# Moved scalings and sink products, a table for the rank comparisons, gated weight loads and more idle products in a sink-window attention with top-1 experts

## The chip, the cores and the metric

The kernel runs on one core of one Trainium2 chip. The metric is the device time of one execution in microseconds (us); a run's figure is the median over its executions, and the document compares medians. One execution was recorded by the hardware profiler; its rows give every duration used below.

## What is computed

The reference is attention with four sink columns and a window of 128, followed by a mixture of experts with one expert per token and a capacity of 80 tokens per expert.

```python
# q, k, v: (4, 8, 768, 64); n_sink = 4, window = 128
scores = scale * np.matmul(q, k.transpose(0, 1, 3, 2))
keep = is_sink | in_window
scores = np.where(keep, scores, -1000000000.0)
a = softmax(scores)                       # max subtracted, sum + 1e-9
x = matmul(a, v) -> (3072, 512)           # tokens by (head, dim)
logits = x @ w_gate                       # 8 experts
expert_idx = argmax(logits); gate_w = softmax(logits)[expert_idx]
for e in range(8):
    tok_idx = tokens of expert e, at most 80, those of the largest gate_w
    h = relu(x[tok_idx] @ w1[e])          # 512 -> 1024
    out[tok_idx] = gate_w[tok_idx, None] * (h @ w2[e])
```

Rows of tokens that are not chosen stay zero.

## The kernel before

The attention part is 48 ticks, each for one pair of query blocks (128 rows) with one pair of heads. Everything in it is in an order written out by hand, the same for all engines: the loop over `n` at line 972 calls, per tick, the scores of tick `n`, the transposes of tick `n - 1`, the weighted sums of tick `n - 2`, and between them the stages of a calendar. `at(key, f, ...)` puts a call into the calendar, `run(n, stage)` runs what is due at that stage of tick `n`. Each engine takes its instructions in that order, so an instruction that waits holds everything behind it on its engine.

In one tick TensorE makes the score products (`scores`, line 581), VectorE masks them and takes the row maxima (`softmax`, lines 599 to 609), ScalarE exponentiates (`exps`, line 619), GpSimd spreads the four sink probabilities into `stk` (`sink_probs`, line 627), and TensorE transposes the probabilities (line 635) and `stk` (`sinks_turn`, line 639). ScalarE copies both out of PSUM (lines 642 and 646), GpSimd masks the copies (lines 654 and 661), and TensorE makes the weighted sums (line 687).

The queries of the first four ticks arrive as four separate transfers (`first_pair`). Each is multiplied by 0.125 on GpSimd (`scale_first`, line 484): numbers 0 and 1 before the ticks, 2 and 3 at the very end of ticks 1 and 2. The gate logits ride on the weighted sums as eight extra value columns. They are made by `value_logits` (line 432) for the values and by `sink_logits` (line 446) for the sink rows. `sink_keep` (line 451) copies the sink part into `vst_raw`, and `round_v` and `split_v` (lines 411, 415) make `vst` from it, which tick 2's weighted sums read.

Gate keys of a token tile are ready some three ticks after its last scores (`gate_terms`, `gate_logits`, `gate_exp`, `gate_hit`, `gate_keys`). `keys_turn` and `keys_keep` lay them out as a row `krow`. A token's rank within its expert is found by comparing its key with all earlier keys, in pieces of up to 768 columns per tile `i`; 60 pieces in all. A piece is done on VectorE (`rank_compare`, lines 827 and 830) or on ScalarE (`rank_sign`, line 845); GpSimd then rescales the ScalarE results (`sign_settle`, line 853), and TensorE sums the other side of each comparison into `cnt` (`rank_count`, line 863). Waiting pieces stand in the list `rank_todo`. In the ticks before, VectorE takes up to two pieces per tick, at most a fifth of the list rounded up, and from tick 32 on ScalarE takes one per tick. Seven pieces are left when the ticks end. They and the last tiles' pieces are done in the tail, lines 1028 to 1117. The tail ends in a loop over what is left (line 1101), with `ot` (GpSimd, line 1095), its sum `os` (VectorE, line 1106) and `base` (GpSimd, line 1107) for the offsets of the experts, and with the sum `rsum` (line 1116) and the subtraction that gives `rank` (line 1117). `keep_warm(n)` issues `n` products whose result nobody reads (line 970).

The selection compares ranks with slots (line 1141), and 24 products (line 1144) turn that into token numbers. Then 14 products that nobody reads follow (line 1161). GpSimd gathers the tokens of expert 0 and 1 from memory (line 1164). For each expert, `tokens` scales the gathered rows on VectorE (line 1201) and transposes them (line 1203), `ffn1` (line 1219) and `ffn2` (line 1240) multiply by the weights, and `rows` writes the output.

Weights come as 32 halves of 1 MB on the SyncE queue, through `load_weight` (line 304). The first 12 go out during the ticks. The loop right behind the attention part (line 1125) asks for four more, numbers 12 to 15: number 12 goes to the last third of the tile `kv`, 13 to 15 to buffers of the pool `wpool3`, whose memory the attention part used before. Number 16 goes to its fourth buffer.

## Time and profile before

| | us |
|---|---|
| median of three runs | 303.65 |
| lowest and highest run | 301.45, 304.17 |
| profiled execution | 305.9 |
| its span, first to last instruction | 304.2 |
| around the span | 1.7 |

The profiled execution is 2.25 us above the median. Its mean granted clock of TensorE is 0.953 of full speed. In the span the first score product starts at 6.30 us, the ticks and the tail reach to the rank at 195.70 us, the first expert's products start at 206.84 us, and the last output transfer is issued at 299.56 us.

### The profile page before, as it was taken

The numbers are of one execution on the slowest core, as the hardware profiler recorded it, in microseconds if no ns is written. First come the engines' busy times: TensorE is split into PE (matmuls) and PEld (weight loads), VectorE is DVE, ScalarE is ACT, GpSimd is POOL, SyncE is SP. The second block draws the span as 40 slices with busy tenths as digits, with TensorE's granted clock in tenths as the row PEclk, the third lists the DMA queues.
The fourth block names the chain that finished last, engine by engine and source line by source line (L and its number), as shares of the span: only waits on it lengthen the run. The fifth ranks groups of instructions, "written<-read, shape, count | busy, mean of one in ns | idle before, by whom it ended". The sixth has DMA issues, their size and how long they took to land.

```text
span 304.2 us, 13249 instructions
## 1 busy us (share of the span) xinstructions
PE 267.5 (88%) x5407; PEld 219.5 (72%) x5407; DVE 165.7 (54%) x508; ACT 165.4 (54%) x652; POOL 138.6 (46%) x365
## 2 busy tenths in 40 slices
PE   8769999999999998999899977478899997998991
PEld 3557787777787766786777756348898986997980
DVE  5666858688688969879878899702301101100001
ACT  1566668887779876989999968300112211211210
POOL 4336557756598654568956747432112201011111
PEclk9989999999999999999999999557999999799997
DMA  7996976194961799999998997891766968358401
GB/s 210 309 346 229 348 320 214 43 364 128 380 214 60 269 410 307 399 400 363 300 401 295 363 412 231 323 340 51 266 210 196 357 227 285 122 202 300 143 26 53
DMA packets 30388, 79.18 MB, mean 260 GB/s; under 512 B 3056, under 2 KB 5104, under 8 KB 30320
## 3 DMA queue, kind: packets, MB, share of 16 engines
q1 hardware_dynamic: 29008, 74.85, 69.3%
q0 software_dynamic: 1024, 2.81, 3.0%
q8 instruction: 45, 0.74, 1.0%
q10 hardware_dynamic: 288, 0.60, 0.5%
q14 instruction: 23, 0.19, 0.2%
HBM read 63.46 MB, written 14.78 MB: 257 GB/s over the span
## 4 chain that ended last, share of the span: by engine, by line
PE 59%; DVE 11%; ACT 10%; issue 6%; DMA 5%; POOL 4%; SPq 3%; POOLq 0%; ACTq 0%; DVEq 0%
PE ph L1219 13%; PE py L1240 13%; PE xp L687 8%; ACT prob L619 7%; PE sc L581 7%; PE pp L635 4%; PE vw L432 3%; DMA out_dram<-zeros 3%; DVE nm L609 2%; DVE sc L602 2%; SPq L875 2%; DMA kv<-in_v_t_dram 2%; PE warm L1161 2%; PE sc L490 2%; PE px L1203 1%
## 5 line engine op out<-in xcount | busy, mean ns | idle before, releaser
L619 ACT ACTIVATE prob<-sc,nm 128x132 f32<-128x132 f32 (+1 forms) x192 | 69.5, 370 | 23.9 <-DVE nm L609 12.8
L581 PE MATMUL sc<-kv,q 64*64 64x196 f32 (+2 forms) x768 | 45.4, 333 | 7.9 <-ACT prob L619 5.1
L602 DVE COPY_PREDICATED sc<-upper,sc 128x256 f32<-128x256 int8 x80 | 33.8, 423 | 20.5 <-PE sc L581 11.2
L609 DVE TENSOR_REDUCE nm<-sc 128x2 f32<-128x264 f32 (+1 forms) x96 | 41.3, 431 | 3.3
L687 PE MATMUL xp<-kv,pt 128*64 128x72 f32 x752 | 41.6, 231 | 0.7 <-issue 0.3
L1269 POOL DMA_INDIRECT out_dram<-y,idx x8 | 7.4, 926 | 68.9 <-ACT y L1258 58.7
L619 ACT ACTIVATION_READ_ACCUMULATOR prob<-sc,nm 128x1 f32 x192 | 38.7, 202 | 0.0
L1205 DVE COPY xs<-px 128x320 f32<-128x320 f32 x8 | 3.9, 492 | 62.6 <-PE px L1203 62.6
L627 POOL CAST stk<-prob 128x32 fp32r<-128x32 f32 x48 | 11.3, 236 | 55.6 <-ACT prob L619 49.3
L581 PEld LDWEIGHTS sc<-kv,q 64*64 64x64 f32 x768 | 22.4, 133 | 19.2 <-ACT prob L619 9.8
L687 PE MATMUL xp<-kv,own 128*64 128x72 f32 x624 | 34.6, 232 | 0.0
L687 PEld LDWEIGHTS xp<-kv,pt 128*64 128x64 f32 x752 | 31.6, 138 | 3.3 <-POOL pt L661 1.0
L635 PE MATMUL pp<-ident,prob 128*128 128x128 f32 x192 | 31.1, 285 | 0.7 <-ACT pt L646 0.7
L1223 ACT ACTIVATE h<-ph 128x320 f32<-128x320 f32 x16 | 7.0, 437 | 42.9 <-PE ph L1219 42.9
L1219 PE MATMUL ph<-xs,w 128*64 128x80 f32 x704 | 29.2, 249 | 1.2 <-DVE xs L1205 1.2
L1219 PEld LDWEIGHTS ph<-xs,w 128*64 128x64 f32 x704 | 28.3, 150 | 1.6 <-DVE xs L1205 1.5
L661 POOL TENSOR_SCALAR_AFFINE_SELECT pt<-pt 128x512 f32<-128x512 f32 (+1 forms) x48 | 26.9, 561 | 3.3
L646 ACT COPY pt<-pp 128x512 f32<-128x512 f32 x48 | 28.0, 583 | 0.5 <-POOL own L654 0.5
L1240 PE MATMUL py<-h,w 128*64 128x80 f32 x640 | 25.1, 234 | 3.0 <-issue 3.0
L687 PEld LDWEIGHTS xp<-kv,own 128*64 128x64 f32 x624 | 25.8, 138 | 2.4 <-POOL own L654 0.2
L654 POOL TENSOR_SCALAR_AFFINE_SELECT own<-pt 128x512 f32<-128x512 f32 (+1 forms) x48 | 27.2, 566 | 0.0
L635 PEld LDWEIGHTS pp<-ident,prob 128*128 128x128 f32 x192 | 20.5, 141 | 8.4 <-ACT pt L646 4.6
(172 smaller groups left out, 486.1 us busy)
## 6 DMA issues: line engine op xcount, KB each, us to landing
w<-in_moe_w_dram SPq DMA_DIRECT2D x21, 1024.0 KB, 7.2
kv<-in_v_t_dram SPq DMA_DIRECT2D x12, 576.0 KB, 8.4
x_rows<-xr SPq DMA_DIRECT2D x22, 292.0 KB, 4.2
vt<-in_vt_t_dram SPq DMA_DIRECT2D x12, 512.0 KB, 6.2
out_dram<-zeros SPq DMA_DIRECT2D x24, 256.0 KB, 7.6
wkv<-in_moe_w_dram SPq DMA_DIRECT2D x6, 1024.0 KB, 7.2
q<-in_q_t_dram SPq DMA_DIRECT2D x11, 512.0 KB, 9.1
kv<-in_moe_w_dram SPq DMA_DIRECT2D x5, 1024.0 KB, 8.2
```

The lines of the kernel that those rows point to most:

```text
L581: pe.matmul(sc[u * D:(u + 1) * D, h, c0 + lo:c0 + hi], qs[g][r, hp, q0:q0 + D], ks[b][r, hp, k0 + lo:k0 + hi], start=True, stop=True, skip ...
L602: ve.copy_predicated(own, upper, sc[:, :, 0:P])
L609: ve.tensor_reduce(out=nm, in_=sc[:, :, lo_c:hi_c], axis=AX.X, op=ALU.max, negate=True)
L619: ac.activation(prob[:, a, h, p0:], sc[:, h, lo_c:hi_c], AF.Exp, bias=nm[:, h:h + 1], scale=1.0, accum_out=ssum[:, n, 2 * hp + h:2 * hp + ...
L627: po.tensor_copy(to[:, 0].bitcast(F32R), wide)
L635: pe.transpose(st[(t, "pp")][:, a, h], prob[:, a, h, SINK:], ident)
L646: ac.copy(pt, st.pop((t, "pp")))
L654: po.affine_select(out=own[:, a0:], in_=pt[:, a0:], pattern=[[0, 2 - a0], [0, 2], [1, P]], compare_op=ALU.is_ge, fill=0.0, base=0, channel ...
L661: po.affine_select(out=pt[:, a0:], in_=pt[:, a0:], pattern=[[0, 2 - a0], [0, 2], [-1, P]], compare_op=ALU.is_gt, fill=0.0, base=0, channel ...
L687: pe.matmul(xp[m * D:(m + 1) * D, a, h * VD:(h + 1) * VD], pr[:, a, h, m * D:(m + 1) * D], val[:, (2 * hp + h) * VD:(2 * hp + h + 1) * VD] ...
L1219: pe.matmul(ph[fc // (HC // 2)][m * D:(m + 1) * D, fc % (HC // 2)], columns(0, e, c, fc * P + m * D), x[:, c], start=(c == 0 and fc % (HC ...
L1240: pe.matmul(to[m * D:(m + 1) * D, dc], columns(1, e, k, dc * P + m * D), h[:, k], start=(k == 0 and (between is not None or dc == 0)), sto ...
```

## The change

Seven edits, all in the order or the place of work; the computed values are the same.

- `scale_first` 2 and 3 move from the end of ticks 1 and 2 to the GpSimd stage of ticks 0 and 1, ahead of that tick's `sink_probs`.
- `sink_logits(0)` moves from tick 1 to the end of tick 0.
- A table `PLAN` fixes for each tick how many pieces ScalarE and VectorE take. VectorE never takes more than one in a tick. ScalarE takes one in ticks 29 to 31 too, and none in ticks 32, 36, 40 and 44. In all, 23 pieces are on ScalarE instead of 20. Nine pieces are left after the ticks instead of seven, and the loop at the end of the tail has five steps instead of four.
- The constants `later` go straight into `parts`. The sum of `ot`, negated, goes into a column of its own in `parts`, right ahead of `rsum`; the step on GpSimd that made `base` is gone.
- Products that nobody reads: four and three more in the tail, two in each of the loop's five steps, three instead of two at its end.
- 16 instead of 14 such products behind the selection.
- The first buffer of `wpool3` is made ahead as `held`.
- The loop that asks for four weights moves into `tokens(0)`, behind the scaling of the first gathered rows and behind a one-column `memset` of `held`, to which weight 13 goes.

```diff
+    PLAN = {14: (0, 1), 15: (0, 1), 16: (0, 1), 17: (0, 1), 18: (0, 1), 19: (0, 1), 20: (0, 1), 21: (0, 1), 22: (0, 1), 23: (0, 1), 24: (0, 1), 25: (0, 1), 26: (0, 1), 27: (0, 1), 28: (0, 1), 29: (1, 1), 30: (1, 1), 31: (1, 1), 32: (0, 1), 33: (1, 1), 34: (1, 1), 35: (1, 1), 36: (0, 1), 37: (1, 1), 38: (1, 1), 39: (1, 1), 40: (0, 1), 41: (1, 1), 42: (1, 1), 43: (1, 1), 44: (0, 1), 45: (1, 1), 46: (1, 1), 47: (1, 1)}
...
-    parts = const.tile([P, NTILE, NPC + 1], F32, name="parts")
+    parts = const.tile([P, NTILE, NPC + 2], F32, name="parts")
...
-    base = parts[:, :, NPC]
+    later = parts[:, :, NPC]
...
-        at(1, scale_first, 2)
-        at(2, scale_first, 3)
-        at((1, "pe end"), sink_logits, 0)
+        at((0, "pool"), scale_first, 2)
+        at((1, "pool"), scale_first, 3)
+        at((0, "pe end"), sink_logits, 0)
...
-                if len(rank_todo) > 1 and n >= 32:
+                for _ in range(PLAN.get(n, (0, 0))[0]):
                     rank_sign()
...
-                left = len(rank_todo)
-                for _ in range(min(left, 2, -(-left // 5))):
+                for _ in range(min(len(rank_todo), PLAN.get(n, (0, 0))[1])):
                     rank_compare()
...
+            keep_warm(4)
             rank_count()
+            keep_warm(3)
             sign_settle()
             keys_turn(i, 1)
...
-                if step == 2:
-                    ve.tensor_reduce(out=os, in_=ot, axis=AX.X, op=ALU.add)
-                    po.tensor_tensor(base, later, os, ALU.subtract)
                 if rank_todo:
                     rank_compare()
                 rank_count()
-                keep_warm(0)
+                keep_warm(2)
                 step += 1
             sign_settle()
             rank_count()
-            keep_warm(2)
+            keep_warm(3)
+            ve.tensor_reduce(out=parts[:, :, NPC + 1], in_=ot, axis=AX.X, op=ALU.add, negate=True)
             ve.tensor_reduce(out=rsum, in_=parts, axis=AX.X, op=ALU.add)
...
-        homes += [(wpool3, m) for m in range(NC)]
-        for n in range(NC):
-            load_weight()
+        held = wpool3.tile([P, 2 * F], F32, tag="w0", name="held", bufs=1)
+        homes += [(None, held)] + [(wpool3, m) for m in range(1, NC)]
...
-            for _ in range(14):
+            for _ in range(16):
...
+            if e == 0:
+
+                ve.memset(held[:, 0:1], 0.0)
+                for n in range(NC):
+                    load_weight()
```

## Rows read from the trace of the kernel before

**Rows 1.** The page's chain that ended last: shares of the span by engine.

```profile
PE 59%; DVE 11%; ACT 10%; issue 6%; DMA 5%; POOL 4%; SPq 3%; POOLq 0%; ACTq 0%; DVEq 0%
```

**Rows 2.** Timeline, first 25 us: start, duration, instruction, idle before it and releaser.

```profile
9.87 0.21 POOL L627 CAST stk<-prob 128x32 fp32r<-128x32 f32 x1 [5.08 <-ACT prob L619]
...
12.42 1.08 PE L446 MATMUL xp<-wg,sv_cols 128*64 128x16 f32 x16
...
13.18 0.41 POOL L484 TENSOR_SCALAR q<-q 128x256 f32<-128x256 f32 x1
...
13.54 0.28 DVE L451 COPY vst_raw<-xp 64x128 f32<-64x128 f32 x1 [1.83 <-PE xp L446]
...
14.82 0.49 DVE L599 COPY_PREDICATED_SCALAR sc<-upper,negc 128x256 f32 x1
...
18.72 0.78 PE L581 MATMUL sc<-kv,q 64*64 64x64 f32 x16 [2.57 <-POOL prob L588]
...
24.84 0.38 ACT L619 ACTIVATE prob<-sc,nm 128x132 f32<-128x132 f32 x1
```

**Rows 3.** DMA issues at 4.56 us: name, count, size, us from issue to landing.

```profile
q<-in_q_t_dram SPq DMA_DIRECT2D x1, 128.0 KB, 6.2
```

**Rows 4.** Windows: stretch, its length, busy us of PE, PEld, DVE, ACT, POOL, PEclk, DMA.

```profile
16.20:18.70 2.50, 0.00 (x0) 0.00 (x0) 1.26 (x4) 2.22 (x11) 0.86 (x5) 1.00 0.99 337
19.84:23.25 3.41, 3.41 (x41) 2.74 (x43) 2.05 (x6) 2.54 (x11) 0.88 (x4) 0.50 0.70 279
187.10:190.50 3.40, 1.28 (x24) 0.90 (x24) 3.26 (x14) 2.75 (x10) 2.64 (x14) 1.00 0.83 293
190.50:204.10 13.60, 9.30 (x78) 5.65 (x79) 5.31 (x16) 2.25 (x7) 5.94 (x18) 0.50 0.95 354
...
207.60:210.90 3.30, 3.30 (x56) 3.30 (x52) 0.00 (x0) 0.00 (x0) 0.96 (x1) 0.50 0.45 118
```

**Rows 5.** Timeline of ticks 30, 31 and 46, 47.

```profile
116.15 1.00 DVE L830 TENSOR_SCALAR_CACHE_REDUCE gt<-krow,keys 128x768 bf16<-128x768 f32 x1
...
118.97 0.37 ACT L619 ACTIVATE prob<-sc,nm 128x132 f32<-128x132 f32 x1 [2.22 <-DVE nm L609]
...
175.96 1.00 DVE L830 TENSOR_SCALAR_CACHE_REDUCE gt<-krow,keys 128x768 bf16<-128x768 f32 x1
...
177.96 0.43 PE L803 MATMUL pk<-ident,keys 128*128 128x128 f32 x2 [1.35 <-DVE keys L758]
```

**Rows 6.** Groups by line on ACT, 108 to 185 us: busy us, mean ns.

```profile
L845 ACT ACTIVATE gts<-krow,under 128x768 bf16<-128x768 f32 x15 | 14.3, 954 | 0.2 <-ACT ex L745 0.2
```

**Rows 7.** Timeline of the tail, the selection and the first expert.

```profile
193.00 0.35 DVE L1106 TENSOR_REDUCE os<-ot 128x24 f32<-128x192 f32 x1 [1.40 <-POOL ot L1095]
...
194.19 1.01 DVE L827 SCALAR_TENSOR_TENSOR gt<-krow,keys,ties 128x768 bf16<-128x768 f32 x1
...
195.43 1.01 PE L970 MATMUL idle_bank<-ones_bf 128*128 128x512 bf16 x2
195.70 0.18 DVE L1117 TENSOR_TENSOR rank<-rsum,cnt 128x24 bf16<-128x24 f32 x1
...
196.53 1.79 PE L1144 MATMUL pi<-picks,krow 128*80 128x40 bf16 x24
...
199.14 5.46 PE L1161 MATMUL warm<-krow 128*80 128x480 bf16 x14 [0.82 <-ACT tab L1154]
...
205.09 0.76 DVE L1201 TENSOR_TENSOR xc<-xg 80x256 f32<-80x256 f32 x2 [6.21 <-DMA xg<-x_rows,idx_in]
...
206.84 6.29 PE L1219 MATMUL ph<-xs,w 128*64 128x80 f32 x128 [0.58 <-DVE xs L1205]
```

**Rows 8.** DMA issues of the gathers at 199.7 us, then of two at 206 to 209.

```profile
xg<-x_rows,idx_in POOLq DMA_INDIRECT x1, 5.3
...
xg<-x_rows,idx_in POOLq DMA_INDIRECT x2, 3.4
```

**Rows 9.** Timeline of PE inside the products of expert 3's second layer.

```profile
258.36 0.36 PE L1240 MATMUL py<-h,w 128*64 128x80 f32 x3 [2.12 <-issue]
```

More of the change, by code (lines that the diff above doesn't have):

```diff
@@ L271, in attention_moe @@
     PIECE, NPC, NGT = 768, 4, 4
+    PLAN = {14: (0, 1), 15: (0, 1), 16: (0, 1), 17: (0, 1), 18: (0, 1), 19: (0, 1), 20: (0, 1), 21: (0, 1), 22: (0, 1), 23: (0, 1), 24: (0, 1), 25: (0, 1), 26: (0, 1), 27: (0, 1), 28: (0, 1), 29: (1, 1), 30: (1, 1), 31: (1, 1), 32: (0, 1), 33: (1, 1), 34: (1, 1), 35: (1, 1), 36: (0, 1), 37: (1, 1), 38: (1, 1), 39: (1, 1), 40: (0, 1), 41: (1, 1), 42: (1, 1), 43: (1, 1), 44: (0, 1), 45: (1, 1), 46: (1, 1), 47: (1, 1)}
     BELOW = 1.0 - 2.0 ** -24
-    SIGNED = [12, 7, 1, 0]
-    parts = const.tile([P, NTILE, NPC + 1], F32, name="parts")
+    SIGNED = [14, 9, 0, 0]
+    parts = const.tile([P, NTILE, NPC + 2], F32, name="parts")
     ve.memset(parts, 0.0)
-    base = parts[:, :, NPC]
+    later = parts[:, :, NPC]
     rsum = const.tile([P, NTILE], F32, name="rsum")
@@ L513, in attention_moe @@
         tile_no = const.tile([P, NTILE], F32, name="tile_no")
-        later = const.tile([P, NTILE], F32, name="later")
         ints = const.tile([P, 3, 2], I32, name="ints")
@@ L1096, in attention_moe @@
             gate_gates(l, 2)
-            os = sm.tile([P, NTILE], F32, name="os", bufs=1)
             print("left", rank_todo)
```

## The prediction

> **What bounds the kernel now.** I read first the chain that ended last, by engine: TensorE has 59% of it, VectorE 11%, ScalarE 10% [rows 1]. No engine is the bound over the whole span, so each edit has to be priced in its own stage. Next I read the timeline of the first 25 us, of two pairs of ticks, and of the stretch from the tail to the first expert's products. The windows add what clock TensorE had in each stretch, and the DMA issues how long the gathers took.
>
> The start loses time in one place above all: the scores of tick 3 begin at 18.72 us after TensorE sat idle for 2.57 us, released by GpSimd [rows 2]. What stands there on GpSimd is the scaling of that tick's queries, at the end of a tick behind everything else. While nothing ran from 16.2 to 18.7 us the clock was still full; from 19.84 to 23.25 it was at its lower level (0.50), with TensorE busy all 3.41 us [rows 4].
>
> The tail ends on VectorE. It stands idle for 1.40 us until GpSimd has made `ot`, sums it in 0.35, and then does the last two pieces of the comparison; the rank follows at 195.70 [rows 7]. The selection's 24 products take 1.79 us at the lower clock, which holds from 190.5 to 204.1 us [rows 4, 7]. Behind them the longest wait is the one for the first gathered rows: VectorE idles 6.21 us until 205.09 [rows 7]. That gather took 5.3 us from issue to landing, two later ones 3.4 [rows 8]. From there to the end TensorE's products are the chain.
>
> **Part by part.** *The start.* `scale_first(2)` now stands on GpSimd ahead of the first `sink_probs`, which ran at 9.87 us. Its queries were issued at 4.56 and took 6.2 us [rows 3], so they land at 10.8. The scaling (0.41, rows 2) ends at 11.2, and `stk` comes 1.3 us later than before. Behind it on GpSimd stand the next tick's `memset` and `stk`. Who waits is TensorE with the transpose of `stk`, and behind that the value logits, because the transposed `stk` must leave the shared bank first. That eats most of the 1.08 us which `sink_logits` leaves free there (12.42 to 13.50): tick 2's scores start perhaps 0.2 us sooner. VectorE gains more. It idled 1.83 us for the sink logits and only then made `vst`, ahead of tick 2's softmax at 14.82 [rows 2]. The transfer into `vst_raw` may hold that copy too, so I take half, 0.9. `sink_logits` itself moves into a place where TensorE runs idle products and waits for tick 0's exponentials.
>
> The scaling of tick 3 goes where GpSimd has nothing urgent, and those scores then wait for TensorE and ScalarE alone: 18.72 less 2.57, and 0.25 for the later sums of tick 0, gives 16.4, so 2.3 us sooner. If the clock then doesn't fall at 19.84, up to half of 3.41 us comes back as well, 1.7. Against that stands a transfer: tick 4's value logits, which stand on ScalarE's path ahead of the exponentials at 24.84, need values whose landing no row here shows. I take the gap alone, **-2.3 us**. The ends are -4.0 (gap and clock) and +1.0 (the later `stk` reaches ScalarE, nothing else is gained).
>
> *The table.* Three more pieces on ScalarE cost 0.95 us each [rows 6], three fewer on VectorE up to 1.00 each. What counts is where. In ticks 30 and 31 the exponentials waited 2.22 us for VectorE's maxima, and a piece of 1.00 at 116.15 stands right in that path [rows 5]. It goes. But ScalarE now has a piece in each of ticks 29, 30 and 31, ahead of its exponentials, and the gaps there cover the pieces only in part: I take -0.4, between -1.0 and +1.0. In tick 46 the piece of 1.00 at 175.96 stands ahead of the keys for which TensorE idled 1.35 us [rows 5]. By the order of the list it becomes one of 128 columns, worth half of 1.00 at least: -0.5, between -0.8 and 0. ScalarE's added piece in tick 47 falls into the time in which it waits for those keys. Ticks 35 and 36 get longer pieces than they had: +0.2, between 0 and +0.5. Together **-0.7 us**, from -1.8 to +1.5.
>
> *The tail.* The stall of 1.40 goes; the 0.35 of the sum goes from the middle to the end and stays on the path. Walked through the list, VectorE's pieces in the tail grow from 5376 to 5632 columns in nine pieces instead of eight: 256 columns at 1.00 per 768 are 0.33, with a start of its own some 0.45. That gives -0.95. On TensorE two idle products per step stand between the sums of `cnt`: at the lower clock one takes 0.50 (1.01 for two, rows 7), at the full one by proportion 0.25. At 0.25 they fit into its idle time (busy 1.28 of 3.40 from 187.1 to 190.5, rows 4), with 0.15 left over at the last step. So **-0.8 us**, from -1.3 to +0.5 with the clock full. The removed `base` step was covered by the pieces on VectorE: 0.
>
> *Selection.* If the idle products keep the clock up, the 24 products of 1.79 us shrink. They follow the comparisons of VectorE, so not by half: **-0.5 us**, from -0.9 to 0. The five products issued right ahead of them (2 + 3) take 1.25 at full clock against 1.01 now; they are covered by `rsum`, the rank and the first slot comparison.
>
> *Weights behind the first rows.* Number 12 doesn't depend on `held` and goes out as before, at the end of the tail. 13 waits for the `memset`, and what stands behind it on SyncE's queue (14 to 16) waits too. Then nothing but the gathers is moving when the rows come, and 5.3 becomes 3.4 [rows 8]: **-1.9 us**, from -1.9 to 0. The `memset` itself stands between the scaling and a copy that waits for TensorE anyway. The four transfers of 1 MB then run from 202 to some 213 us and collide with the next two gathers (5.3 again instead of 3.4), whose rows the second and third expert need several us later. Weight 13 is first needed after two further experts, more than 30 us on.
>
> The 16 idle products stand ahead of the first transposes on TensorE. Now 14 take 5.46, 0.39 each [rows 7]; 16 take 6.2 at that pace, 3.1 at full clock. With rank and selection 1.3 us sooner they begin at 197.8 and end at 201.0 or 204.1. The first rows are scaled at about 202.2 (gather at 198.4, 3.4, half of 0.76). At full clock they cost nothing; at the lower one they hold the rows by 1.9.
>
> *The experts.* The first layer of expert 0 took 6.29 us, with the clock at its lower level for 3.30 us of it [rows 4, 7]. TensorE fell to that level after a stretch in which it ran the last idle products and then waited for rows. A like wait (201.0 to 202.2) is left, so I count 0, and -1.6 as the far end. The Trainium skill speaks for more: its page "TensorE: Matmul & The Clock Gate", Part 1, puts the lower level down to idleness, and by that a TensorE that only pauses would hold the full one. The sum by it would be 1.6 us lower. Here the trace differs, since the engine was not idle throughout before this fall.
>
> A stop of 2.12 us without a releaser stands inside expert 3's products [rows 9], while weights and an output were on their way. Moved transfers can move or add such a stop: 0 taken, -2 to +2. Here the Trainium skill speaks against a cost: its page "Runtime: NRT & Kernel Launch", section "Instruction fetch mechanics", has the fetch of instructions mostly hidden. If that is what stopped TensorE, the row says otherwise, and the forecast goes by the row.
>
> **Sum.** -2.3 - 0.7 - 0.8 - 0.5 - 1.9 = -6.2. From the profiled 305.9 (span 304.2 and 1.7 around it) this gives 299.7. That execution lies 2.25 above the median, 303.65, which carries over to 297.45: 297.5.
>
> **Rivals.**
>
> A. *Only one weight is held back.* Numbers 14 to 16 have buffers that are free early, and if SyncE's order is made by readiness they go out ahead of 13, as now. For: nothing in the diff ties them to the `memset`. Against: they are asked for behind it, on one queue. With 3 MB instead of 5 around the gather, about half of the 1.9 is left, 0.9: 298.5.
>
> B. *The start gives nothing.* GpSimd's new wait for the queries, or the values of tick 4, take the 2.3 back. For: 10.8 lies behind 9.87. Against: the idle 2.57 is one order away from being used. 299.8.
>
> C. *The idle products run at the lower clock, and the path waits for them (slower).* The clock falls as it did at 190.5, or earlier, and each product costs 0.50. Up to the last sum of `cnt` there are 15, 7.5 us. TensorE's idle time there is 2.1 up to 190.5 and some 3.9 after (4.9 to 195.4, less 1.0 of sums that remain of the 9.30 when 1.01, 1.79 and 5.46 are taken off; rows 4, 7). About half of these 6.0 lies in waits for pieces that can't be used ahead of time, so the rank comes 3.0 us late instead of 0.8 early. The five ahead of the selection add 1.5 (2.5 against 1.01), the two more behind it 0.8, of which 1.0 was free before: +4.3 at the first rows in place of -3.2. 303.65 - 3.0 + 4.3 = 305.0. It decides from 3.0 us on, what start and table give. For: TensorE was busy just 1.28 of 3.40 before the present fall. Against: the added products fill that very stretch.
>
> **Chances.** Forecast 0.5, A 0.2, B 0.2, C 0.1. The range from 294.5 (clock kept in the start or in expert 0) to 301.5 (B with a worse table, or one more stop among the experts) leaves out C and about one in ten besides. One per cent, 3 us, is about what a measurement of this kernel can tell from no change (the three runs spread over 2.7). Faster by over 1% is below 300.6: nearly all of the forecast, most of A, 0.6 of B, 0.76 in all. Within 1%: the rest of these and half of C, 0.16. Slower: 0.08.
>
> **What would show it.** The start: scores of tick 3 at about 16.4, exponentials of tick 4 at about 22.5, full clock around 20 us. The table: no wait near 2 us ahead of tick 31's exponentials. The tail: no stall at the sum of `ot`, rank 0.8 sooner from the last tick on. The clock: full from 187 to the gather. The gather: 3.4 us from issue to landing, SyncE's weights behind the first scaling. The forecast is wrong if the idle products take 0.4 to 0.5 each, if 14 to 16 go out early, or if stops among the experts come to more than 2 us more or less than now.

## The result, and the profile after

The changed kernel took **295.03 us** (median of 4 executions, 292.95 to 298.49) against 303.81 for the kernel before in the same comparison (4 executions, 301.45 to 304.17). The ratio is 0.968, 95% interval 0.963 to 0.973: of 303.65 us that is 8.1 to 11.3 less, where the forecast was 6.2 less. (Ratios leave out executions more than 1.5% above the fastest of the same kernel; medians are over all.)

That was not the last word on the size. Three later comparisons of the same kernel, told below, gave 0.980, 0.981 and 0.982. Over all four, 20 executions of it lie between 292.95 and 300.41 with a median of 297.4; 89 of the kernel before, one of 970.56 left out, have 303.6. So the change is worth about 6 us (4.4 to 8.8 by the medians of the four comparisons), and single executions of the changed kernel lie up to 4.5 us from their median. Much of what follows is about that spread.

The profile after is of the execution of 292.95 us (span 291.2, mean granted clock 0.992). The chain that ended last, by engine, for [rows 1]:

```profile
PE 58%; ACT 11%; DVE 11%; DMA 9%; issue 6%; POOL 1%; SPq 1%; POOLq 0%; ACTq 0%; DVEq 0%
```

GpSimd has gone from 4% to 1%: its late scaling no longer stands in the chain. The timeline of the start, for [rows 2]:

```profile
7.13 1.10 PE L447 MATMUL xp<-wg,sv_cols 128*64 128x16 f32 x16
...
10.01 0.41 POOL L485 TENSOR_SCALAR q<-q 128x256 f32<-128x256 f32 x1 [5.50 <-DMA q<-in_q_t_dram]
10.36 0.21 POOL L627 CAST stk<-prob 128x32 fp32r<-128x32 f32 x1
...
12.06 0.28 DVE L452 COPY vst_raw<-xp 64x128 f32<-64x128 f32 x1 [0.22 <-DMA vst_raw<-in_vs_t_dram]
...
15.36 0.45 PE L581 MATMUL sc<-kv,q 64*64 64x64 f32 x8
...
21.40 0.38 ACT L619 ACTIVATE prob<-sc,nm 128x132 f32<-128x132 f32 x1
```

The queries of tick 2 landed 5.4 us after issue (6.2 in [rows 3]), so `stk` came at 10.36, only 0.49 later than before. The scores of tick 3 begin at 15.36 without an idle wait, and tick 4's exponentials at 21.40 instead of 24.84. The windows show the clock, for [rows 4]:

```profile
19.84:23.25 3.41, 3.41 (x78) 2.82 (x74) 2.38 (x5) 2.48 (x13) 2.11 (x6) 1.00 0.89 298
187.10:190.50 3.40, 3.40 (x37) 1.72 (x35) 2.94 (x8) 0.66 (x2) 2.35 (x8) 0.55 0.75 247
190.50:204.10 13.60, 10.48 (x176) 8.07 (x175) 3.12 (x11) 0.79 (x3) 4.53 (x6) 0.99 0.81 300
```

It is full in the start, falls once near 187, and is back before the selection ends; before it was low from 190.5 to 204.1. Ticks 31 and 47 by their exponentials, for [rows 5]:

```profile
114.52 0.37 ACT L619 ACTIVATE prob<-sc,nm 128x132 f32<-128x132 f32 x1 [0.18 <-POOL pt L661]
...
172.66 0.43 PE L803 MATMUL pk<-ident,keys 128*128 128x128 f32 x2 [0.71 <-DVE keys L758]
...
174.05 0.37 ACT L619 ACTIVATE prob<-sc,nm 128x132 f32<-128x132 f32 x1 [0.55 <-DVE nm L609]
```

The wait of 2.22 us ahead of tick 31 is 0.18. Tail, selection and first expert, for [rows 7], and then the gathers' issues, for [rows 8]:

```profile
188.89 0.34 DVE L1113 TENSOR_REDUCE parts<-ot 128x24 f32<-128x192 f32 x1
...
189.89 0.18 DVE L1115 TENSOR_TENSOR rank<-rsum,cnt 128x24 bf16<-128x24 f32 x1
...
191.16 1.08 PE L1141 MATMUL pi<-picks,krow 128*80 128x40 bf16 x24
...
193.03 3.40 PE L1158 MATMUL warm<-krow 128*80 128x480 bf16 x16 [0.79 <-ACT tab L1151]
...
197.70 0.76 DVE L1198 TENSOR_TENSOR xc<-xg 80x256 f32<-80x256 f32 x2 [4.93 <-DMA xg<-x_rows,idx_in]
...
199.46 4.65 PE L1221 MATMUL ph<-xs,w 128*64 128x80 f32 x128 [0.59 <-DVE xs L1207]
```

```profile
xg<-x_rows,idx_in POOLq DMA_INDIRECT x1, 4.1
...
held<-in_moe_w_dram SPq DMA_DIRECT2D x1, 1024.0 KB, 5.5
xg<-x_rows,idx_in POOLq DMA_INDIRECT x2, 6.3
```

No stall at the sum of `ot`. The gather took 4.1 us and not 3.4; three of the four weights had gone out before it (at 186.75, 187.21 and 189.57) and only `held` waited.

By stage, the two profiles of before and the four of the changed kernel (three from below). The columns: tick 4's exponentials; from there to tick 31's; to tick 47's; to the rank; to the first transposes of expert 0; to the end of the span; and expert 0's first layer.

| profile (execution, us) | tick 4 | to 31 | to 47 | to rank | to rows | to end | layer 1 |
|---|---|---|---|---|---|---|---|
| before (305.9) | 24.84 | 94.13 | 60.38 | 16.35 | 9.91 | 98.56 | 6.29 |
| before, again (305.7) | 23.95 | 94.41 | 60.39 | 16.43 | 10.27 | 98.52 | 7.38 |
| changed (292.95) | 21.40 | 93.12 | 59.53 | 15.84 | 8.29 | 93.06 | 4.65 |
| changed, ctl (298.45) | 23.70 | 93.06 | 60.36 | 15.86 | 8.98 | 94.77 | 6.29 |
| changed, ctl2 (295.73) | 21.20 | 93.12 | 60.33 | 16.01 | 8.79 | 94.57 | 6.16 |
| changed, ctl3 (296.13) | 22.55 | 93.12 | 59.52 | 15.84 | 8.96 | 94.42 | 6.29 |

Some columns are the same within 0.3 us in every profile of a kernel (to 31, to the rank), others differ by 2 us within one kernel (tick 4, the experts). Only the first sort can be priced from one pair of profiles. Both profiles of before are some 2 us above its median, so the last column but one overstates the experts' share.

### The profile page after: what moved, and what is told of

It reads as the page before. It is cut to its first block, busy times and chain, and to the rows that moved or that the text cites. A ratio compares the mean times of both kernels' runs of the same rounds, so it can differ in the third digit from the quotient of the medians.

```text
span 291.2 us, 13292 instructions
## 1 busy us (share of the span) xinstructions
PE 265.0 (91%) x5427; PEld 215.9 (74%) x5427; DVE 163.3 (56%) x503; ACT 167.7 (58%) x658; POOL 140.7 (48%) x367
## 4 chain that ended last, share of the span: by engine, by line
PE 58%; ACT 11%; DVE 11%; DMA 9%; issue 6%; POOL 1%; SPq 1%; POOLq 0%; ACTq 0%; DVEq 0%
PE py L1242 13%; PE ph L1221 12%; ACT prob L619 8%; PE sc L581 7%; PE xp L687 7%; DMA out_dram<-zeros 6%; PE pp L635 5%; PE vw L433 4%; DVE nm L609 2%; DVE sc L602 2%; DMA kv<-in_v_t_dram 2%; PE sc L491 2%; DMA xg<-x_rows,idx_in 1%; ACT pt L646 1%; PE px L1205 1%
## 5 line engine op out<-in xcount | busy, mean ns | idle before, releaser
L687 PE MATMUL xp<-kv,pt 128*64 128x72 f32 x752 | 40.9, 229 | 0.8 <-issue 0.4
L687 PEld LDWEIGHTS xp<-kv,pt 128*64 128x64 f32 x752 | 30.9, 137 | 2.7 <-POOL pt L661 1.1
L1221 PE MATMUL ph<-xs,w 128*64 128x80 f32 x704 | 25.9, 233 | 1.2 <-DVE xs L1207 1.2
L1221 PEld LDWEIGHTS ph<-xs,w 128*64 128x64 f32 x704 | 25.1, 137 | 1.6 <-DVE xs L1207 1.5
L845 ACT ACTIVATE gts<-krow,under 128x768 bf16<-128x768 f32 x23 | 21.8, 948 | 0.5 <-ACT ex L745 0.2
```

Source lines behind the costliest of these rows:

```text
L687: pe.matmul(xp[m * D:(m + 1) * D, a, h * VD:(h + 1) * VD], pr[:, a, h, m * D:(m + 1) * D], val[:, (2 * hp + h) * VD:(2 * hp + h + 1) * VD] ...
L845: ac.activation(gt, krow[:, c * PIECE:(c + 1) * PIECE], AF.Sign, bias=under[:, i:i + 1], scale=BELOW, accum_out=ra)
L1221: pe.matmul(ph[fc // (HC // 2)][m * D:(m + 1) * D, fc % (HC // 2)], columns(0, e, c, fc * P + m * D), x[:, c], start=(c == 0 and fc % (HC ...
```

## Experiments

**The kernels again.** ctl, ctl2 and ctl3 are the changed kernel, before2 is the kernel before, without an edit.

> The changed kernel once more, unchanged. Theory (a gain of some 9 us made of start 3.4, table 1.5 to 1.9, tail with selection 1.0, a full clock in expert 0 of 1.6, the rest chance among the experts): the ratio to the kernel before is 0.968 to 0.975 again, and everything up to the first gather falls within 0.5 us of its first profile (exponentials of tick 4 at 21.4, of tick 47 at 174.05, gather issued at 193.6); the stops without a releaser among the experts lie elsewhere or have another length. Rival (the stops among the experts were cured by the change, not by chance): they come to under 2 us again, at the same places.

> The changed kernel a third time. Ten executions of it so far lie between 292.95 and 300.16 with a median of 297.3, against 303.3 for before. Theory (the change is worth about 6, and the first comparison's 9 to 10 had executions in it in which the clock happened not to fall and few stops happened): median of this batch 296.0 to 298.5, ratio 0.975 to 0.982. Rival (the first comparison was the typical one): 293.5 to 295.5, ratio 0.966 to 0.972.

> The kernel before, profiled a second time, for a table by stage that doesn't rest on one execution of it. Theory: up to the first rows it repeats (exponentials of tick 4 at 24.8 to 25.3, 154.5 from there to tick 47's, 16.35 to the rank, 9 to 10 to the first rows), and only the stretch from the first rows to the end, where the clock and the stops fall differently, is elsewhere, by up to 4 us (98.6 in the first profile). Rival (the stretch of the experts was made shorter by the change): 97.5 to 99 there again, against 92.2 to 96.3 in the eight profiles with the change or parts of it.

Measured: ctl 298.9 (6 executions), ratio 0.980, interval 0.972 to 0.989; ctl2 297.75 (6), 0.981, 0.974 to 0.988; before2 304.8 (12), 1.003. The first expectation for ctl fell: its ratio is not 0.968 to 0.975, its tick 4 came at 23.70, 2.3 later than in the first profile, and tick 47 was 3.1 later. ctl2's theory (about 6 us, 0.975 to 0.982) came true. The windows of ctl (busy us of PE, clock, DMA share) and its timeline there:

```profile
9.00:12.40 3.40, 1.76 (x23) 1.00 1.07 257
12.40:15.80 3.40, 3.40 (x48) 0.50 1.07 393
15.80:19.20 3.40, 3.40 (x44) 0.50 1.02 312
203.50:207.00 3.50, 3.50 (x60) 0.51 0.92 318
```

```profile
10.49 0.41 POOL L485 TENSOR_SCALAR q<-q 128x256 f32<-128x256 f32 x1 [6.02 <-DMA q<-in_q_t_dram]
...
11.44 0.30 PE L639 MATMUL ts<-ident,stk 128*64 128x128 f32 x1 [0.76 <-POOL prob L588]
```

Here the same queries took 5.9 us. GpSimd waited for them ahead of `stk`, TensorE waited 0.76 for GpSimd, and the clock was at its lower level from 12.4 to 19.2 us: some 2 us of the start's gain gone. That the wait brings the low clock is not shown: u_start, told next, fell at 12.5 without such a wait. The second low stretch, from 203.5, is expert 0. The rival for before2, 97.5 to 99 in the experts, came true. So the 4 us between the two kernels there are not the chance of one profile (see the end).

**The start.** u_start takes the three edits of the start out of the changed kernel, b_start puts them alone into the kernel before, and start_b is the changed kernel with the scalings one place later, behind the sink probabilities.

```
u_start   +  at(1, scale_first, 2)      at(2, scale_first, 3)
          +  at((1, "pe end"), sink_logits, 0)
b_start   +  at((0, "pool"), scale_first, 2)      at((1, "pool"), scale_first, 3)
          +  at((0, "pe end"), sink_logits, 0)
start_b   -  at((0, "pool"), scale_first, 2)      at((1, "pool"), scale_first, 3)
          +  at((0, "act mid"), scale_first, 2)   at((1, "act mid"), scale_first, 3)
```

> The changed kernel with the three edits of the start undone: scalings of ticks 2 and 3 and the sink logits where they were. Theory: exponentials of tick 4 at 24.8 again (+3.4), the clock falls near 20 us again, and the 3.4 us stay to the end of the ticks (exponentials of tick 47 at 177.5) and to the end of the kernel: 1.0 to 1.2% slower than the changed kernel. Rival (the forecast's term: the gap alone is worth 2.3, and the clock's part comes back anyway): exponentials of tick 4 at 23.7, 0.8% slower. Second rival (what the start gains is lost again behind some later transfer): tick 47 at most 1 us later than in the changed kernel.

> The kernel before with the three edits of the start alone. Theory: exponentials of tick 4 at 21.4 to 22.1 where the clock stays full in the start and 23.3 to 23.7 where it falls, against 24.8 before, the rest of the ticks as before (154.5 to tick 47); the median 2 to 3 us below before, 0.7 to 1.0%. Rival (the forecast's ends): -4.0 or +1.0.

> The changed kernel with the two scalings right behind the sink probabilities of ticks 0 and 1 instead of ahead of them. Theory (where the queries of tick 2 land late, GpSimd holds the sink probabilities of tick 0, TensorE stands idle for up to 0.8 us, and the clock falls right behind that, which costs some 2.3 us in such executions): the sums of tick 0 begin on GpSimd near 9.9 whatever the queries do, the scores of tick 2 come 0.3 to 0.8 sooner, tick 4's exponentials at 20.6 to 21.4, the clock full up to 25 us; the median of the whole 0.2 to 0.8% below the changed kernel's. Rival (the fall of the clock in the start comes from elsewhere): low clock near 12 to 20 us in its profile too, and no difference in the median.

Measured: u_start has tick 4 at 25.19 with the clock low from 12.5 to 22.7, and 300.5 us (0.988, 0.984 to 0.993), beside 298.9 for ctl in the same comparison. b_start has it at 23.82, with the clock low from 12.3 to 19.2, and 0.992 (0.988 to 0.997): 1.0 to 3.7 us, but only 0.4 by the medians over all executions (302.8 against 303.3). The gap itself is gone there (TensorE has no wait of its length ahead of tick 3); the clock decides how much of it is kept. In start_b the sums of tick 0 no longer wait (`stk` at 9.92), and yet tick 4 comes at 22.07:

```profile
20.75 1.11 PE L433 MATMUL vw<-wg,vt 128*64 128x16 f32 x32 [0.22 <-DMA vt<-in_vt_t_dram]
21.90 0.27 ACT L439 COPY kv<-vw 128x128 f32<-128x128 f32 x1 [1.22 <-PE vw L433]
```

What is late next is the value transfer that the forecast named as its doubt: it lands at 20.70. The clock stayed full before tick 4 here, and in the three later kernels with the scalings in this place (best1 to best3); in the thirteen profiles with the scalings ahead of the sink probabilities it fell before 20 us in seven. Four profiles don't prove that this order is the cure. Its time, 295.1 (0.973, 0.969 to 0.978), is not to be told from the changed kernel's.

**The table.** u_table goes back to the rule of before.

```
-  SIGNED = [14, 9, 0, 0]
+  SIGNED = [12, 7, 1, 0]      (pieces on ScalarE by column of the list; constants go by it)
...
-  for _ in range(PLAN.get(n, (0, 0))[0]):
+  if len(rank_todo) > 1 and n >= 32:
       rank_sign()
...
-  for _ in range(min(len(rank_todo), PLAN.get(n, (0, 0))[1])):
+  left = len(rank_todo)
+  for _ in range(min(left, 2, -(-left // 5))):
```

> The changed kernel with the rule of before in place of the table. Theory: the wait ahead of tick 31's exponentials comes back (tick 31 about 1.4 later relative to tick 4), and tick 47 is 1.5 to 2.0 later than in the changed kernel (about 175.8); the tail starts later by as much and runs one step of pieces shorter: whole kernel 1.0 to 2.0 us slower, 0.3 to 0.7%. Rival (the forecast's term): 0.7 us, 0.2%. Second rival (the ticks gain, but one more piece in the tail gives it back): gather issued within 0.5 us of the changed kernel's 193.6.

Measured: 94.18 from tick 4 to tick 31 instead of 93.06 to 93.12, 60.67 on to tick 47, and 300.4 us (0.991, 0.987 to 0.995). The piece and the wait are back:

```profile
112.82 1.01 DVE L830 TENSOR_SCALAR_CACHE_REDUCE gt<-krow,keys 128x768 bf16<-128x768 f32 x1
...
115.64 0.37 ACT L619 ACTIVATE prob<-sc,nm 128x132 f32<-128x132 f32 x1 [2.21 <-DVE nm L609]
```

The theory holds at its lower end: the table gives 1.1 up to tick 31, the same against each profile of the changed kernel, and 0.3 to 1.1 behind. The time says 1.5 us (298.9 for ctl in the same comparison) to 3 (297.4 over all executions of the changed kernel).

**The tail.** u_offsets puts the sum of offsets back into the third step; u_idle takes the added idle products out; no_last takes out only the three right ahead of the selection.

```
u_offsets  +  if step == 2:
           +      ve.tensor_reduce(out=parts[:, :, NPC + 1], in_=ot, ..., negate=True)
           -  ve.tensor_reduce(out=parts[:, :, NPC + 1], in_=ot, ..., negate=True)   (ahead of rsum)
u_idle     -  keep_warm(4)   keep_warm(3)   keep_warm(2)   keep_warm(3)   range(16)
           +                                keep_warm(0)   keep_warm(2)   range(14)
no_last    -  keep_warm(3)      (the last of the four)
```

> The changed kernel with the sum of offsets back in the third step of the tail's loop. Theory: VectorE waits there for the products on GpSimd as before, by 0.5 to 1.4 us, and the rank comes 0.3 to 1.0 us later relative to tick 47 (16.2 to 16.8 after its exponentials in place of 15.85). Rival (with five steps in place of four the products are ready by then): within 0.2 of 15.85. In the whole time at most 0.4%.

> The changed kernel without the added idle products of the tail (0, 0, 0 and 2 in place of 4, 3, 2 a step and 3; 14 ahead of the first rows in place of 16). Theory (the idle products are what keeps the clock up there, which is worth about 0.6 in the selection and 1.6 in expert 0): the lower clock holds from about 186 to 200 us as before, the 24 products of the selection take 1.7 in place of 1.08, the first layer of expert 0 6.0 to 6.3 in place of 4.65; 0.6 to 0.9% slower. Rival (they do nothing that the shorter tail would not do): the clock as in the changed kernel, first layer 4.65, no difference. Second rival (they cost): the rank comes earlier than in the changed kernel by over 0.5 us.

> The changed kernel without the three idle products that stand right ahead of the selection (those in the steps stay). Theory (at full clock they are free, but while the clock is still low they take 0.5 each and with the two ahead of them hold the selection: 1.9 from the rank to its first product in the profiles with a longer low stretch, 0.9 to 1.1 in the others): 0.83 to 1.1 from the rank to the first product whatever the clock does. Its 24 products then take 1.1 to 1.8. In the time 0 to 0.5 us less, not to be told from none. Rival (they bring the clock back): the low clock lasts until the gather, the 24 products take 1.8, and expert 0's first layer 6 us.

Measured: with the sum in the middle VectorE waited 0.74 for `ot`, and the rank came 16.77 after tick 47, 0.8 to 0.9 later than in the changed kernel, as its theory had it. Without the added idle products (u_idle) the rank comes at 15.86, as with them; the clock is low from 184.3 to 198.0 and the 24 products take 1.79, but expert 0's first layer is 4.65, and the time is 296.0 (0.978, 0.971 to 0.985). So the theory for u_idle fell: the products don't decide expert 0, and in the time they give nothing that shows. What takes their gain away stands in start_b's timeline, beside u_idle's:

```profile
190.99 2.29 PE L970 MATMUL idle_bank<-ones_bf 128*128 128x512 bf16 x5
...
193.08 1.51 PE L1141 MATMUL pi<-picks,krow 128*80 128x40 bf16 x24
```

```profile
190.19 1.01 PE L970 MATMUL idle_bank<-ones_bf 128*128 128x512 bf16 x2
...
191.73 1.79 PE L1139 MATMUL pi<-picks,krow 128*80 128x40 bf16 x24 [0.53 <-DVE krow L1136]
```

Where the clock is still low when the five last idle products run (start_b, warm24, u_table, u_offsets, best1, no_late), they take 2.1 to 2.3 and hold the selection, which ends 2.8 to 3.4 us after the rank. Where it is full or comes back while they run (the changed kernel's four profiles, u_start, u_weights, gate_all, best2), they take 1.2 to 2.0, and it ends 2.1 to 2.4 after. Without them (before, u_idle) it is 2.62. Without the last three alone (no_last) it was 0.83 + 1.79, the same 2.62, with the clock low from 188.9 to 199.2. So its theory held for the way to the first product, the rival for the clock and the 1.79; expert 0 had 4.65 all the same.

**The weights.** u_weights loads them as before; gate_all holds all four buffers.

```
u_weights  -  held = wpool3.tile(...)      (and the memset and loop in tokens)
           +  homes += [(wpool3, m) for m in range(NC)]
           +  for n in range(NC): load_weight()
gate_all   +  held = [wpool3.tile(..., tag=f"w{m}", name=f"held{m}") for m in range(NC)]
           +  homes += [(None, t) for t in held]
           +  for t in held: ve.memset(t[:, 0:1], 0.0)
```

> The changed kernel with the weights loaded as before: no buffer held, all four asked for in the tail. Theory (only one transfer of four was moved, and it was moved onto the next gathers): 3 or 4 MB are on their way around the first gather, which takes 4.5 to 5.3 us from issue to its rows in place of 4.1 to 5.0; 0 to 0.8 us lost there, which can't be told from no difference in the time. Rival (the forecast's step: all the weights behind the rows): the gather 1.9 us longer and the kernel 0.6% slower.

> The changed kernel with all four buffers held by the memset behind the first rows' scaling, so that numbers 13 to 16 really go out behind it. Theory (the forecast's step was right in its price, only the change doesn't do it): nothing but gathers moves when the first rows are fetched, and they land 3.4 us after issue in place of 4.1 to 5.0: the first products of expert 0 0.7 to 1.5 us sooner relative to the rank. Of this nothing need be left at the end: 4 MB collide with gathers 2 and 3, which then take 6 to 7 us. Rival (the gather's time is its own and not the weights'): 4.1 or more as in the changed kernel. Second rival (the later weights are then late for expert 3): a wait for number 13 to 16 of over 1 us among the experts.

Measured, the first gather of u_weights, and then that of gate_all with what follows it:

```profile
xg<-x_rows,idx_in POOLq DMA_INDIRECT x1, 6.1
```

```profile
xg<-x_rows,idx_in POOLq DMA_INDIRECT x1, 3.5
...
held<-in_moe_w_dram SPq DMA_DIRECT2D x4, 1024.0 KB, 10.0
xg<-x_rows,idx_in POOLq DMA_INDIRECT x2, 8.1
```

The 6.1 of u_weights lies above the 4.5 to 5.3 of its theory, 1.1 to 2.0 over the changed kernel's and so near the rival's 1.9. gate_all agrees with the forecast's price: with all four weights held the rows come in 3.5 us, and it has the shortest way of all from the rank to the rows, 7.45 (8.3 to 9.0 in the changed kernel, 10.27 in u_weights). But its time is 298.5 (0.983, 0.978 to 0.988) and that of u_weights 297.7 (0.976, 0.971 to 0.982): no gain in the one, no loss in the other that shows. In gate_all the four transfers meet the next two gathers (8.1), and TensorE stopped for 1.55 us at 219.0, a place at which no other profile stops. What else is moving is not the whole of a gather's time, though. With three weights asked for ahead as in the changed kernel, the first gather took 3.4 to 3.6 us in start_b, warm24, best1 and no_late, and 5.9 in best2. start_b's:

```profile
xg<-x_rows,idx_in POOLq DMA_INDIRECT x1, 3.4
```

In the first four it went out 4.2 to 4.8 us after the third weight, in the changed kernel's four profiles 3.5 to 4.1 after. That this is the reason is not shown: u_table and u_offsets had 4.7 and 4.5, and their gathers took 4.5 all the same.

**Expert 0's clock.** warm24 has 24 idle products ahead of the first rows. best1 joins it with start_b and moves tick 4's value logits (and the transfer that needs their buffer) to tick 5; best2 adds three idle products in the tail, best3 leaves out the last three.

```
warm24  -  for _ in range(16):
        +  for _ in range(24):
best1   -  n = 4 if g == 1 else 4 * g - 2
        +  n = 5 if g == 1 else 4 * g - 2      (and load_vt of g == 2 at 5)
best2   +  keep_warm(3)      (behind the sums of cnt that follow the owed offsets)
best3   -  keep_warm(3)      (the last of the four)
```

> The changed kernel with 24 idle products ahead of the first rows in place of 16. Theory (the clock falls in expert 0 right behind a stretch in which TensorE stood idle for 2 to 3.8 us waiting for the first rows, so filling that stretch keeps it up): first layer of expert 0 4.65 whatever the execution, no lower clock between 196 and 212 us, the first transposes not held (8 products of 0.21 us at full clock are 1.7, and the idle time ahead of the rows was 1.75 to 3.8); median 0.5 to 1.0 us lower. Rival (the fall there doesn't hang on that idle time): 6 us again for the first layer in one profile of two, no difference. Second rival (the products run at the lower clock and hold the rows): first transposes over 0.5 us later relative to the gather's landing.

> The changed kernel with the scalings of ticks 2 and 3 right behind the sink probabilities, tick 4's value logits moved one tick on (with the transfer of the next values), and 24 idle products ahead of the first rows. Theory: in the start nothing waits for the queries of tick 2 or the values of tick 4 any more, exponentials of tick 4 at 20.5 to 21.3 and the clock full; expert 0's first layer 4.65; median 294.5 to 296 against 297.4, and a narrower spread. Rival (the start is bound by what comes behind, another transfer): tick 8's exponentials no sooner than in the changed kernel.

> As best1, with three more idle products between the last offsets' products and the first step of the tail, where TensorE stood idle ahead of the fall at 187. Theory (that idle time is what the clock falls on): full clock from 176 to the end of the experts, the selection's 24 products 1.1, 1.1 from the rank to their first; 0 to 0.8 us below best1. Rival (the fall at 187 comes all the same): as best1, or 0.3 later at the rank for the products that stand ahead of the sums of cnt.

> As best1, without the three idle products right ahead of the selection. Theory: 0 to 0.5 us below best1, 294 to 296. Rival (they bring the clock back): 0 to 0.5 above best1.

Measured in warm24, and in ctl for comparison:

```profile
195.29 5.02 PE L1158 MATMUL warm<-krow 128*80 128x480 bf16 x24 [0.79 <-ACT tab L1151]
200.14 0.44 PE L1205 MATMUL px<-ident,xc 80*128 80x80 f32 x4
201.17 4.65 PE L1221 MATMUL ph<-xs,w 128*64 128x80 f32 x128 [0.58 <-DVE xs L1207]
```

```profile
195.91 3.40 PE L1158 MATMUL warm<-krow 128*80 128x480 bf16 x16 [0.79 <-ACT tab L1151]
201.96 0.69 PE L1205 MATMUL px<-ident,xc 80*128 80x80 f32 x4 [2.66 <-DVE xc L1198]
203.24 6.29 PE L1221 MATMUL ph<-xs,w 128*64 128x80 f32 x128 [0.58 <-DVE xs L1207]
```

All four kernels with 24 products had 4.65; with 16 it was 4.65 in six profiles of twelve and 5.98 to 7.39 in the other six.

The idle time of TensorE ahead of the first transposes sorts the 20 profiles of this document in part. With 0 to 0.45 us of it (the four with 24, u_idle, no_last) the layer was 4.65 in all six, and with 2.4 to 3.8 (ctl, ctl2, ctl3, u_start, u_weights) the clock fell in all five. Between, from 1.0 to 2.2, it fell in four (before, before2, b_start, gate_all) and stayed full in five. A rival was not tried: three of the four kernels with 24 products had the clock low for some 6.8 us just ahead, around the selection, and the six with 14 or 16 products and a low stretch of that length or more (u_table, u_idle, u_offsets, start_b, no_last, no_late) had 4.65 as well. So it is not shown that the eight more products keep the clock up.

warm24 took 296.7 (0.980), best1 296.5 (0.973, 0.967 to 0.979), best2 297.5 (0.977), best3 296.7 (0.976). The start of best1 and best2 did reach tick 4 at 20.83 and 20.50, but then the next value logits waited for their transfer, in best1 so:

```profile
27.93 1.11 PE L433 MATMUL vw<-wg,vt 128*64 128x16 f32 x32 [1.19 <-DMA vt<-in_vt_t_dram]
```

The clock fell at 30, and tick 8 came at 37.05 and 36.97 (34.76 in the changed kernel's first profile, 37.05 in ctl): the rival. None of these is shown to beat the changed kernel.

**The stops.** no_late loads no half weight from number 17 on, so that the later experts compute with expert 1's weights.

```
+  if n >= 17:
+      wtiles[(which, e, half)] = wtiles[(which, 1, half)]
+      return
```

> The changed kernel without the transfers of the half weights from number 17 on: experts from the second half of expert 3's second layer on (first layers from expert 4 on) compute with expert 1's weights, which are still in their buffers. The stops without a releaser stood at the same counts of TensorE's products from the start in every kernel: 3587, 4098, 4225, 4480, 4862, spaced by 127 or 128 or a multiple. Theory (at these places TensorE waits for its next block of instructions, which stands behind the weights' transfers): the counts 4098 and 4862 are crossed without a stop over 0.3 us, those before 3715, where weights still move, may keep theirs; 2 to 3 us less from the first rows to the end than in the control. Rival (a stop belongs to the place, whatever moves): 0.8 to 1.4 us at 4098 and at 4862 as before.

> The changed kernel on the same chip, as control for the one without late weights. Theory: stops of 0.8 to 1.5 us at the 4098th product or at the 4862nd or both, median 296 to 298.5. Rival (they are chance without a place): stops over 0.6 at other counts.

Measured: ctl3 297.4 (4 executions, 0.982, 0.978 to 0.987), no_late 292.8 (0.959). ctl3 stopped for 0.92 at TensorE's 3587th product, 1.05 at the 4098th and 1.49 at the 4862nd. The windows of ctl3 up to the second and third (in brackets the products so far), and those of no_late across the same two places:

```profile
0.00:233.60 233.60, 214.19 (x4098) 0.98 0.82 289
0.00:263.90 263.90, 243.26 (x4862) 0.98 0.82 285
```

```profile
229.90:234.50 4.60, 4.60 (x135) 1.00 0.07 26
259.50:264.10 4.60, 4.60 (x135) 1.00 0.02 4
```

With the DMA share at 0.07 and 0.02 TensorE crossed both places without a pause, and the way from the first rows to the end was 89.1 us (94.4 in ctl3, of which 1.6 is expert 0's clock). A stop of 0.57 stayed at the 3460th product, at 210.3 us, right behind the last weight. The theory holds.

## Why the prediction was right and where it was wrong

*The sum.* 297.5 was forecast with a range from 294.5; the first comparison gave 303.65 times 0.968, 294.0, just below it. The step that failed is the one that put the clock of expert 0 and the stops at 0 ("so I count 0", "0 taken") and the start at its gap alone, with a range that let the clock be kept "in the start or in expert 0". In the profile of that comparison all three fell on the good side at once (its execution is 2.1 us below the comparison's median). Expert 0's first layer took 4.65 us instead of 6.29, 1.6 less where 0 was counted. Tick 4 came 3.4 sooner where 2.3 was counted. The stops over 0.5 us came to 1.4 in all instead of 3.2, 1.8 less where 0 was counted; in ctl2 they came to 2.1, in ctl3 to 3.5 and in ctl to 3.7. Together that is 4.6 us more than forecast, of which the weights, below, took some back. Why three executions of that comparison were all low isn't settled.

The median of all 20 executions is 297.4. That this meets the likeliest time to 0.1 us is in part luck: over the table's profiles the rank table gave 1.6 us where 0.7 was taken, the way from the rank to the first rows 1.3 where selection and weights had 2.4, and the experts gave some that the forecast didn't count and that isn't explained (see the end).

*The start, -2.3.* The gap went as said. "I take the gap alone" was the wrong way to put the rest: whether the clock falls is not one cost but differs by execution. Tick 4 gained 2.2 on average over the table's profiles (22.2 against 24.4), between 0.25 and 3.6. The later `stk` that the forecast priced at 1.3 came 0.3 to 1.1 later than in the first profile of before. In ctl TensorE's wait for it stands right ahead of the clock's fall; as u_start and warm24 fell at 12.5 and 12.8 without it, it is not the only way to that fall.

*The table, -0.7.* Too small. The pieces on ScalarE in ticks 29 to 31 cost nothing that shows: 1.1 up to tick 31, where -0.4 was taken, right at the far end of -1.0. Behind, 0 to 0.9 against -0.3.

*The tail, -0.8.* Measured -0.5 from tick 47 to the rank, and -0.8 to -0.9 for the moved sum alone (u_offsets), which would leave 0.4 for the longer pieces, near the 0.45 priced; no run tried them alone. The stall was priced at its full 1.40, and in u_offsets it is 0.74.

*Selection, -0.5.* In the changed kernel's four profiles the clock was back in time, and it is -0.2 to -0.5 (2.1 to 2.4 for 2.62); in the variants where it was not, +0.2 to +0.8. Rival C's mechanism is real, then, but only in the five products right ahead of the selection; those in the steps are covered. How often an execution has the one or the other is not known beyond these profiles.

*Weights, -1.9.* Here the mechanism itself was wrong, to the other side: "what stands behind it on SyncE's queue (14 to 16) waits too". It doesn't. The three with free buffers stand ahead of `held` in SyncE's order, so rival A's mechanism came, and with it the forecast's own sign of being wrong, "if 14 to 16 go out early". This cost part of the term, so it is not why the first comparison came out below the range. The gather took 4.1 to 5.0 us, 5.3 to 5.7 before: 0.9 less on average, the half that A said. The price itself agrees with gate_all's 3.5, with the reserve that four kernels with three weights ahead had 3.4 to 3.6 too.

*Expert 0, 0.* "A like wait (201.0 to 202.2) is left, so I count 0" held in ctl, ctl2 and ctl3 (6.16 to 6.29) and not in the first profile (4.65). The wait ahead of the first transposes was 1.75 us there and 2.4 to 2.7 in the other three. The forecast's objection, that TensorE had not been idle throughout before the fall, doesn't carry far: of the 20 profiles the six with a wait of 0 to 0.45 us kept 4.65, and the five with 2.4 to 3.8 lost it. The Trainium skill's page "TensorE: Matmul & The Clock Gate", Part 1, puts the lower level down to idleness. These two ends agree with it; between them the wait alone doesn't decide, since gate_all fell after 1.14 and u_table kept the clock after 2.18.

*Stops, 0 with 2 either way.* Right: 1.4 to 3.7 us after, 2.4 to 3.2 in the two profiles of before. Rival B (the start gives nothing) is refuted by tick 4, which came at 22.5 on average in the thirteen profiles with the scalings ahead of the sink probabilities and at 24.7 in the three without the edits; in the time b_start's ratio says the same (0.992, 0.988 to 0.997), its medians hardly.

*Open.* In the experts 98.5 us in both profiles of before stand against 93.1 to 94.8 in the changed kernel. Clock and stops explain part; both executions were also 2 us above the median. The change shifts TensorE's instruction stream by 20 products ahead of the experts, and so the places at which it stops. That is not the explanation: u_idle, without these 20 products, has 93.6. Nor does any other edit taken out alone bring 98.5 back (92.5 to 96.1 in u_start, u_table, u_offsets and u_weights), and b_start, the kernel before with the start alone, has 96.8. The cause stays open.

## What to carry to other kernels

Price a clock fall as something that happens in a share of the executions, and look at several profiles of the kernel before to see which stages repeat to 0.1 us and which don't. An order that is made by readiness holds back only what itself waits: to keep several transfers behind one event, each needs the dependence. Idle products are free only where nothing urgent stands behind them at the lower clock too.

## What the hardware showed beside

TensorE's stops without a releaser stand at fixed counts of products from the start, whatever the kernel: 3460 (start_b, u_offsets, no_late), 3587 (nine profiles), 3715 (gate_all), 3843 (the four with 24 idle products), 4098 (twelve profiles), 4225 (u_idle), 4352 (b_start), 4480 (u_idle, before, before2), 4862 (thirteen profiles), to within two. They are 127.5 apart or a multiple of it; each product here has its weight load, so that is 255 instructions. u_idle, with 20 products fewer ahead, and ctl:

```profile
0.00:236.50 236.50, 216.44 (x4225) 0.97 0.84 294
0.00:248.10 248.10, 226.47 (x4480) 0.97 0.83 290
0.00:263.90 263.90, 240.92 (x4862) 0.97 0.82 285
```

```profile
0.00:235.80 235.80, 215.95 (x4098) 0.97 0.81 286
0.00:266.20 266.20, 245.02 (x4862) 0.97 0.81 283
```

The instruction queue in the profile's list of DMA queues moved 45 packets of 0.74 MB in all, 16 KB each. The Trainium skill's page "Runtime: NRT & Kernel Launch", section "Instruction fetch mechanics", has engines refill their instructions in blocks of 16 KiB, 256 instructions, at a cost that is "mostly hidden". The spacing agrees. The cost agrees in no_late, where almost nothing moved, and not where weights were on their way: 0.6 to 2.1 us at a crossing. That it is the fetch which waits, the traces bear out a second time: every one of these stops, in all profiles, ended 1.26 to 1.62 us after a packet of that queue had landed (47 stops over 0.5 us; at crossings without one it was 1.1 to 6.6). That it hangs on the transfers is shown by no_late.

Two stops were long, 2.12 us in the first profile of before [rows 9] and 2.00 in best1. Behind each, within 1.2 us, the clock fell to its lower level in the middle of the experts' products; behind the shorter ones it did not.
